# Which idle memory an attention kernel lends to its Exp results, and when it takes it back

## The chip, the cores and the metric

The kernel runs on one core of one Trainium2 chip. The metric is the device time of one execution in microseconds (us). The engines are named as in the profile: PE is TensorE, ACT is ScalarE, DVE is VectorE, POOL is GpSimd, SP is SyncE, whose queue issues most DMAs.

## The reference

Two layers, each an attention block and a feed-forward block with residuals, on x of 2048 tokens by 512, bfloat16. Attention has 32 heads of 16 columns; the feed-forward width is 1792. Both layers use the same weights.

```
def _A_ref(x, wqkv, wo):                     # H = 32, Dh = 16
    q, k, v = split(x @ wqkv)
    scores = einsum("bhqd,bhkd->bhqk", q, k) * Dh ** -0.5
    return reshape(einsum("bhqk,bhkd->bhqd", softmax(scores), v)) @ wo

def _B_ref(x, w1, w2):
    return silu(x @ w1) @ w2

x = x + _A_ref(_layernorm(x), A_wqkv, A_wo)
x = x + _B_ref(_layernorm(x), B_w1, B_w2)
x = x + _A_ref(_layernorm(x), A_wqkv, A_wo)
x = x + _B_ref(_layernorm(x), B_w1, B_w2)
```

## The kernel before

**Tiling.** Queries are cut into four chunks c of 512 tokens, heads into eight blocks hb of four heads. A *segment* is one (layer L, chunk, head block): its scores for 16 blocks of 128 keys. A *tile* is one key block of a segment for two of its four heads, a 128 x 1024 piece of scores in one of three PSUM slots. There are 2 x 4 x 8 x 16 x 2 = 2048 tiles, numbered in order; the planner starts a new "rule" letter every 16 tiles (`STRETCH`).

**One tile.** PE computes its scores (L1306, in the profile `slot<-QT,KT`; 32-row layout), two tiles or one in an issue group. Then there are two ways. (1) ACT takes the Exp from the slot into an Exp buffer (L1530, 128 x 1024 bfloat16), and PE multiplies it with V (L1383, `q_ps<-p,v`, column layout). (2) DVE makes a first power-of-two approximation from the slot (L1564), and three more terms are made from it by adding constants to the bits, on POOL (L1625) or DVE (L1598, called shifts below); the sum of the four terms stands for the Exp. Such a tile needs four buffers and four value matmuls per head instead of one. So a tile can be moved from ACT to DVE, POOL and PE.

**Segments and layers.** The 74 segments are: 32 of the first layer; ten "old" ones of the second layer, which use only the keys of the first three chunks (12 key blocks), because the fourth chunk's feed-forward is not done yet; then the "new" ones that add the missing 4 key blocks, between whole segments of chunk 1; then the rest of chunks 1, 2 and 3. When an old segment closes, DVE copies its unfinished sum out of PSUM (L1199) into `o_old`, rows of 1024 columns in `v_flat`, which held V of the first layer; the new segment of the same head block later rescales it (L499) and adds it (L1203).

**V and its memory.** V of the first layer lies in `v_flat`, V of the second in `x_flat` (8704 columns each, 2176 for a chunk). A V piece (`v_piece`) is 16 matmuls (four per 128 columns of the contraction, in four column groups), an eviction on DVE (L379) and a memset of ones on POOL. `next_pieces` queues the four V pieces of a chunk behind its layer norm once the first layer's feed-forward of this chunk is done.

**The order of the work.** `Flow` is a planner in the kernel's Python. It keeps a clock for each engine, with fixed costs for each kind of instruction, and writes all engines' instructions in the order of its clocks. Background work (keys, queries, V, projections, feed-forward) is cut into `Piece`s of steps with a tile number at which they are due, in four queues; a piece starts only when all pieces in its `after` list are done, and a piece that can't start holds the ones behind it in its queue. PE's turn (`pe_turn`) chooses between scores, values and a background step; when none is possible it may issue a filler matmul (L1423).

**Buffers.** The planner starts with 14 Exp buffers (`NB`). The list `lent` adds others: (first segment, last segment, memory). When segment i begins, `lend` adds the buffers of entries that start at i, and removes those that end at i from the free list; one that is still in use is not given back. ACT's and DVE's turns take the buffer that comes free first. Whether a tile goes to DVE is decided in `want_dve`: among others, when at least `spare` buffers would be free.

```
if sum(b[0] <= at + 600 for b in self.bufs) - self.owed() < self.spare:
    return False
```

**Rule letters.** `RULES` is a string of 128 letters, one for each 16 tiles. Each stands in `KINDS` for seven settings: `spare`, how many value groups may wait (`many`), at how few free buffers values go first (`few`), how many shifts may be queued (`behind`), a factor on the rate of background work (`hurry`), and when DVE helps POOL with shifts (`help`, `wait`). The letter r, with `spare` 99, sends no tile to DVE and speeds background work by 1.5.

Of the kernel before, what the change touches and what calls it, by code (L numbers as in the profile page):

```python
# [20 lines left out]
def kernel(  # L21
# [17 lines left out]
    H = 32  # L39
# [4 lines left out]
    NQC = S // 512  # L44
    FT = F // P
    HB = H // 4
# [3 lines left out]
    VW = DH + 1  # L50
# [77 lines left out]
    v_flat, x_flat = (xpool.tile([P, TT * H * VW], BF16, name=f"v{i}") for i in range(2))  # L128
# [57 lines left out]
    def o_kept(seg):  # L186
        return o_old[seg.hb] if seg.c != 1 else o_more[MORE.index(seg.hb)]
# [46 lines left out]
    def turn(out, in_):  # L234
        turns.append((T_ISSUE, T_LAND))
        nc.sync.dma_start_transpose(out=out, in_=in_)
# [52 lines left out]
    def ln_pieces(c, cell, after):  # L289

        def rs():
            cell["mvb"], cell["rstd"] = ln_scalars(cell["st"])

        def apply(i):
            xn = cell["hT"][:, i, :]
            ln_apply(cell["mvb"], cell["rstd"], i, 4 * c + i, xn)
            turn(xnTs[c][:, :, i * P : (i + 1) * P], xn)

        first = Piece([("sp", 0, rs, "")], after, T_POOL)
        free = [first] + [freed] * (c == 0 and cell.get("L") == 1)  # L300
        return [first, Piece([dve(460, lambda i=i: apply(i), "l") for i in range(4)], free)]
# [27 lines left out]
    def k_piece(L, c, hb):  # L329
        cell = {}  # L330

        def out():
            st = cell["st"] = stpool.tile([P, 512], BF16, name="kq", tag="kq")
            nc.vector.tensor_copy(out=st[:], in_=cell["ps"][:, :])  # L334
            move(kept_q[L, hb, c, :, :], st[:])

        p = Piece(four(
            lambda cts: k_mm(c, hb, cell["ps"][:, :], cts),
            lambda: bank(cell, "k_ps"),
        ) + [dve(700, out, "c"), dve(424, lambda: k_out(c, hb, cell["st"][:]), "l")])  # L340
        p.key = (L, c, hb)
        p.store = Piece([])
        return p
# [31 lines left out]
    def v_piece(tt, L):  # L375
        cell = {}

        def out():
            nc.vector.tensor_copy(  # L379
                out=vs[L][:, tt, :, 0:DH], in_=cell["ps"][:, :].rearrange("p (h d) -> p h d", d=DH)  # L380
            )
            if L:
                ones_v(L, tt, tt + 1)
            v_made.add((L, tt))

        p = Piece(four(
            lambda cts: v_mm(tt, cell["ps"][:, :], cts),
            lambda: bank(cell, "v_ps"),
        ) + [dve(700, out, "c")])
        p.value = (L, tt)  # L390
        return p
# [138 lines left out]
    def heads_piece(oT, seg, attn):  # L530
        alone = seg.c < 2 and (seg.L == 1 or seg.hb < 2)
        alone = alone or (seg.L, seg.c, seg.hb) == (1, NQC - 1, HB - 2)
        k = 0 if alone else seg.hb % 2
        if k == 0:
            at_cell["at"] = opool.tile([P, 4, 2, P], BF16, name="at", tag="at")
        at = at_cell["at"]
        turn(at[:, :, k, :], oT[:])
        if not alone and k == 0:
            return None
        n = 4 * (k + 1)  # L540
        heads = at[:].rearrange("p t s (j w) -> p t (s j) w", j=4)[:, :, 0:n, :]
        cell = {}

        def first():
            cell["rec"] = heads_rec(heads)

        def second():
            heads_mul(heads, cell["rec"], seg.hb - k, attn)

        return Piece([dve(252 if k == 0 else 354, first), dve(536 if k == 0 else 757, second, "l")])  # L550
# [64 lines left out]
    def ffn_pieces(c, emit_out, ln, after):  # L615
# [33 lines left out]
            ))  # L649
        return pieces  # L650

    normed = {}

    def next_pieces(c, L, ln, after):
        ln = ln_pieces(c, ln, after)
        v = [v_piece(4 * c + tq, L) for tq in range(4)]
        normed[c] = ln[-1]
        v[0].after = [ln[-1]]
        return ln + v

    def tail_mm(slots, tq, k):
# [155 lines left out]
    n_old = NQC * HB + HB + len(MORE) - 1  # L817
# [5 lines left out]
    def due(pieces, n):  # L823
        for p in pieces:
            p.due = n
        return pieces
# [88 lines left out]
    def spare(at):  # L915
        made = {}

        def views():
            if not made:
                made["v"] = at()  # L920
            return made["v"]

        return views

    def rows(t, lo, hi):
        return lambda: [
            t[:, 1024 * k : 1024 * k + 1024].rearrange("p (a b) -> p a b", a=2)
            for k in range(lo, hi)
        ]
# [9 lines left out]
    def key_rows():  # L939
        assert with_q[1, NQC - 1, HB - 1].done  # L940
        return [wkq[:, ct, 0 : 2 * D].rearrange("p (a b) -> p a b", a=2) for ct in range(CT)]

    done = n_old + 2 + 2 * HB
    keyed = max(s.i for s in segs if s.kind == "new" and s.c == 0) + 1
    lent = [
        (0, HB, spare(rows(x_flat, 0, 3))),
        (0, 2 * HB, spare(rows(x_flat, 3, 5))),
        (0, 3 * HB, spare(rows(x_flat, 5, 7))),
        (0, 4 * HB, spare(rows(x_flat, 7, 8))),
        (n_old + 3, n_old + HB, spare(idle_hidden)),  # L950
        (n_old + 4, 99, spare(wv_rows)),
        (keyed, 99, spare(key_rows)),
        (done, 99, spare(rows(v_flat, 0, 8))),
    ]

    class Flow:
# [234 lines left out]
        def close(self):  # L1191

            seg = segs[self.open]
            if self.heads is not None:
                self.force(self.heads)
            at = max(self.dve, self.close_at)
            oT = None
            if seg.kind == "old":
                nc.vector.tensor_copy(out=o_kept(seg), in_=self.o_ps[:])  # L1199
            else:  # L1200
                oT = opool.tile([P, 512], BF16, name="oT", tag="oT")
                if seg.kind == "new":
                    nc.vector.tensor_tensor(  # L1203
                        out=oT[:], in0=o_kept(seg), in1=self.o_ps[:], op=ALU.add
                    )
                else:
                    nc.vector.tensor_copy(out=oT[:], in_=self.o_ps[:])
            self.dve = at + 604
            self.o_free = at + 799
            self.close_at = None  # L1210
            self.open += 1
            if self.open == len(segs):
                return oT
            if oT is not None:
                at_ = (seg.L, seg.c)
                if seg.hb == 0:
                    for piece in ends.get((seg.L, seg.c - 2), []):
                        self.force(piece)
                    attns[at_] = apool.tile([P, 4, D], BF16, name="attn", tag="attn")
                piece = self.heads = heads_piece(oT, seg, attns[at_])  # L1220
                land = self.landed(at + 700)
                if piece is not None:
                    piece.ready = land
                    self.bg.append(piece)
                if at_ == (1, NQC - 1) and seg.hb == HB - 3:

                    def early(attn=attns[at_]):
                        for tq in range(4):
                            turn(
                                xnTs[1][:, 0 : CT - 1, tq * P : (tq + 1) * P],  # L1230
                                attn[:, tq, 0 : (CT - 1) * P],
                            )

                    self.turned = Piece([("sp", 0, early, "")], piece)
                    self.qs[2].append(self.turned)
                if seg is more_last:
                    freed.done = True
                if seg.hb == HB - 1:
                    ln = {"L": seg.L}
                    new = epilogue_pieces(seg.c, attns[at_], ln)  # L1240
                    new[0].after = [p for p in (piece, self.fed) if p is not None]
                    ends[at_] = new[-1:]
                    new += ffn_pieces(seg.c, seg.L == 1, ln, new[-1])
                    self.fed = new[-1]
                    if seg.L == 0:
                        new += next_pieces(seg.c, 1, ln, new[-1])
                        if seg.c == NQC - 1:
                            new.append(k_piece(1, seg.c, 0))
                            v_end.append(new[-1])
                    end = {(0, 2): 30, (0, 3): n_old + 1, (1, 0): 66, (1, 1): 69}.get(  # L1250
                        at_, min(seg.i + 1 + HB, len(segs) - 1)
                    )
                    self.qs[1] += self.known(due(new, first[end] - 8))
            return oT
# [413 lines left out]
    }  # L1668
    RULES = (
        "mmmmddddddddddddlllllllldddddddduuuuuuuujjjjuuuullllllllllllllll"  # L1670
        "jjjjjjjjeeeeeeeewwwwwwwwooooooooAAAAAAAAyyyyyyyysssslllloooooooo"
    )
    TAU, NEAR, URGENT, HARD = 700, 300, 4000, 6000
    FROM, TO, EARLY = 0, 99, 300
# [155 lines left out]
```

## Time and profile before

| | us |
|---|---|
| three runs, median | 1598.44 |
| lowest and highest of them | 1597.79, 1599.42 |
| the profiled execution, its own time | 1597.37 |
| its span, first to last instruction | 1595.6 |

The profile has a page of totals, a table of groups of equal instructions (line, engine, operation, tiles, shapes, count | busy us, mean ns of one | idle us before them, and what ended that idle time), lists of waits (who waited for whom: us in total, times, longest us), busy times by stretches of the span, and a timeline of each engine. On ACT, DVE and PE the recorded durations of consecutive instructions overlap, so the step from one start to the next is shorter than a duration. DMA is no matter here:

```profile
HBM read 17.20 MB, written 11.27 MB: 18 GB/s over the span
```

The prediction divides the tiles into eight stages of 256. In the profile of before the first Exp starts at 31.6 us and the last ends at 1551.5; the stages begin at 31.6, 217.8, 404.4, 592.4, 787.7, 989.8, 1181.9 and 1367.7 us.

### The profile page before, as it was taken

What the parts mean: (1) busy time and instruction counts of PE and PEld (TensorE: products, weight loads), DVE (VectorE), ACT (ScalarE), POOL (GpSimd) and SP (SyncE); (2) the same over time, 40 slices, a digit from 0 to 9 for tenths busy, and PEclk for the clock granted to TensorE, in tenths of its full rate; (3) what the DMA queues carried; (4) which work ended last, traced back from release to release, by engine and by line L of the source; (5) the groups of instructions that cost most, each with busy time, mean ns of one, the idle gap of its engine ahead of it and who ended that gap; (6) DMA issues with size and microseconds to landing.
All of it is one profiled execution on the core that took longest, in us unless ns stands there. A gap on an engine that the chain in (4) does not pass through costs nothing.

```text
span 1595.6 us, 41986 instructions
## 1 busy us (share of the span) xinstructions
PE 1523.0 (95%) x17024; PEld 482.7 (30%) x17030; DVE 1253.2 (79%) x1588; ACT 1549.9 (97%) x1761; POOL 1283.5 (80%) x1335
## 2 busy tenths in 40 slices
PE   8999999999999999999999999999999999999998
PEld 3222222223322332233233332232222323323333
DVE  7888888887887777667997458888887698787864
ACT  6999999999999999999999999999999999999993
POOL 3889899997888887767787556897999899888980
PEclk9999999999999999999999999999999999999999
DMA  5011101100110011001111011112100110020010
GB/s 198 21 40 37 30 24 30 24 8 21 30 24 11 11 25 43 11 11 34 57 53 34 14 27 40 27 42 49 27 14 16 33 27 14 16 42 12 17 25 14
DMA packets 105747, 49.28 MB, mean 31 GB/s; under 512 B 79024, under 2 KB 105040, under 8 KB 105552
## 3 DMA queue, kind: packets, MB, share of 16 engines
q1 hardware_dynamic: 103536, 45.51, 11.1%
q8 instruction: 133, 2.18, 0.6%
q10 hardware_dynamic: 2016, 1.08, 0.2%
q14 instruction: 62, 0.51, 0.1%
HBM read 17.20 MB, written 11.27 MB: 18 GB/s over the span
## 4 chain that ended last, share of the span: by engine, by line
PE 51%; ACT 25%; DVE 13%; issue 6%; POOL 3%; DMA 1%; ACTq 0%; DVEq 0%; POOLq 0%
PE slot L1306 18%; ACT p L1530 17%; PE q_ps L1383 14%; PE y_ps L312 7%; PE h_ps L312 4%; ACT v L1530 3%; DVE p L1564 3%; PE k_ps L312 3%; ACT t_sb L595 2%; POOL p L1625 2%; DVE hT L599 1%; PE v_ps L312 1%; ACT wkq L1530 1%; DVE v L1564 1%; DVE p L1598 1%
## 5 line engine op out<-in xcount | busy, mean ns | idle before, releaser
L1530 ACT ACTIVATE p<-slot 128x1024 bf16<-128x1024 f32 x1164 | 1163.5, 1204 | 5.4 <-PE slot L1306 4.6
L1625 POOL TENSOR_TENSOR p<-p,steps 128x512 int32<-128x512 int32 x648 | 684.5, 1078 | 170.5 <-DVE p L1564 151.1
L1306 PE MATMUL slot<-QT,KT 32*128 32x512 bf16 x4096 | 589.5, 381 | 37.8 <-ACT p L1530 24.0
L1383 PE MATMUL q_ps<-p,v 128*17 128x512 bf16 x5002 | 564.3, 381 | 5.5 <-POOL p L1625 1.8
L1564 DVE TENSOR_SCALAR p<-slot 128x1024 uint16<-128x1024 f32 x329 | 401.1, 1219 | 109.0 <-PE slot L1306 93.9
L1306 PEld LDWEIGHTS <-KT 32*128 32x128 bf16 x4096 | 197.7, 91 | 591.2 <-issue 585.1
L1530 ACT ACTIVATE v<-slot 128x1024 bf16<-128x1024 f32 x280 | 316.9, 1203 | 0.3 <-PE slot L1306 0.2
L1383 PEld LDWEIGHTS <-v 128*17 128x17 bf16 x6844 | 161.4, 88 | 283.5 <-issue 230.8
L1383 PE MATMUL q_ps<-v,v 128*17 128x512 bf16 x1214 | 193.1, 381 | 1.0 <-DVE v L1598 0.6
L1625 POOL TENSOR_TENSOR v<-p,steps 128x512 int32<-128x512 int32 x143 | 152.8, 1075 | 25.2 <-DVE p L1564 22.7
L1625 POOL TENSOR_TENSOR p<-v,steps 128x512 int32<-128x512 int32 x145 | 154.4, 1083 | 12.3 <-DVE v L1564 11.0
L312 PE MATMUL h_ps<-xnT,w_sb 128*32 128x512 bf16 x1568 | 132.5, 384 | 7.5 <-DVE hT L599 5.8
L1564 DVE TENSOR_SCALAR v<-slot 128x1024 uint16<-128x1024 f32 x82 | 100.0, 1219 | 25.7 <-PE slot L1306 24.4
L312 PE MATMUL y_ps<-w_sb,hT 128*32 128x512 bf16 x1568 | 116.9, 382 | 0.3
L599 DVE SCALAR_TENSOR_TENSOR hT<-t_sb,h_ps 128x512 bf16<-128x512 f32 x98 | 66.8, 682 | 43.3 <-ACT t_sb L595 43.0
L1530 ACT ACTIVATE wkq<-slot 128x1024 bf16<-128x1024 f32 x80 | 93.5, 1212 | 0.2 <-PE slot L1306 0.2
L312 PE MATMUL k_ps<-xnT,wkq 128*32 128x512 bf16 x960 | 78.6, 384 | 0.7 <-DVE kq L334 0.4
L595 ACT ACTIVATE t_sb<-h_ps 128x512 f32<-128x512 f32 x98 | 75.9, 774 | 0.0
L1598 DVE TENSOR_SCALAR p<-p 128x1024 int16<-128x1024 int16 x98 | 69.6, 713 | 1.0
L1625 POOL TENSOR_TENSOR v<-v,steps 128x512 int32<-128x512 int32 x52 | 56.0, 1081 | 8.8 <-DVE v L1564 8.8
L423 DVE SCALAR_TENSOR_TENSOR QT<-qc,cols,q_ps 128x512 bf16<-128x512 bf16 x74 | 54.7, 739 | 9.6 <-PE q_ps L312 9.0
L1383 PE MATMUL q_ps<-wkq,v 128*17 128x512 bf16 x336 | 60.7, 382 | 0.1
(163 smaller groups left out, 1446.1 us busy)
## 6 DMA issues: line engine op xcount, KB each, us to landing
qc<-kept_q SPq DMA_DIRECT2D x70, 112.0 KB, 2.0
kept_q<-kq SPq DMA_DIRECT2D x60, 128.0 KB, 1.7
w_sb<-in_B_w_dram SPq DMA_DIRECT2D x2, 1792.0 KB, 13.3
out_dram<-x_sb SPq DMA_DIRECT2D x15, 128.0 KB, 1.7
x_sb<-in_A_x_dram SPq DMA_DIRECT2D x3, 512.0 KB, 6.5
old_q<-QT SPq DMA_DIRECT2D x10, 128.0 KB, 1.7
q_was<-old_q SPq DMA_DIRECT2D x10, 128.0 KB, 2.1
at<-oT SPq DMA_TRANSPOSE x63, 2.3
```

The costliest lines, as they stand in the source:

```text
L312: nc.tensor.matmul(ps[g, :], lhsT=lhsT[:, g], rhs=rhs, start=start, stop=stop, skip_group_check=True)
L423: nc.vector.scalar_tensor_tensor(out=dst, in0=qc[:], scalar=own, in1=ps, op0=ALU.mult, op1=ALU.add)
L595: nc.scalar.activation(t_sb, ps, ACT.Tanh, scale=0.5)
L599: nc.vector.scalar_tensor_tensor(out=hT[:, ft, :], in0=t_sb, scalar=1.0, in1=ps, op0=ALU.add, op1=ALU.mult)
L1306: nc.tensor.matmul(self.slots[k][:, jj, :], lhsT=KT[32 * j : 32 * j + KR, t.seg.hb, t.kt * P : (t.kt + 1) * P], rhs=t.seg.QT[32 * j : 32 * ...
L1383: nc.tensor.matmul(self.o_ps[32 * j : 32 * j + VW, :], lhsT=vs[seg.L][:, t.kt, 4 * seg.hb + j, :], rhs=buf[:, jj, :], start=not seg.opened ...
L1530: nc.scalar.activation(buf[:].rearrange("p a b -> p (a b)"), self.slots[x.slot][:].rearrange("p a b -> p (a b)"), ACT.Exp, scale=float(SCALE),
L1564: nc.vector.tensor_scalar(out=whole.bitcast(U16), in0=self.slots[x.slot][:].rearrange("p a b -> p (a b)"), scalar1=float(UNIT), scalar2=fl ...
L1598: nc.vector.tensor_scalar(out=x.bufs[k][1][:].rearrange("p a b -> p (a b)").bitcast(I16), in0=whole.bitcast(I16), scalar1=SHIFTS[k], scala ...
L1625: nc.gpsimd.tensor_tensor(out=b1.bitcast(I32), in0=b0.bitcast(I32), in1=steps32[:, k : k + 1].to_broadcast([P, 512]), op=ALU.add,)
```

## The change

It has four parts.

1. *Lending in the first layer.* Before, eight rows of 1024 columns of `x_flat` were lent from the start and taken back three, two, two and one at the segments 8, 16, 24 and 32. Now each chunk's part of `x_flat` gives two rows, taken back at the segments 12, 20, 28 and 38 (`wanted`). A gate, a `Piece` without steps, stands in the `after` list of each chunk's first V piece, and is set done when the segment `wanted[c]` becomes the open one, that is when all values of the segments before it are issued.
2. *Old results' rows.* When the last segment of the first layer closes, the rows 1 to 7 of `v_flat` are lent; row hb is taken back at the start of segment 32 + hb, whose old result goes there. When a new segment of chunk 0 closes, its row is lent again. Before, all eight rows were lent at segment 59.
3. *The idle hidden tile.* The seven buffers in `hT`'s memory, lent at segment 44, are taken back at segment 52 in place of 49.
4. *Rule letters.* 64 of the 128 letters are set anew, in pairs, 36 of them for tiles up to 1024.

The number of buffers in hand is then 22 to tile 384, 20 to 640, 18 to 896, 16 to 1024 and 23 just after it (then one less with each segment to 38, where three more go), where it was 22 to tile 256, 19 to 512, 17 to 768, 15 to 1024 and 14 after it.

```diff
+    wanted = [HB * (c + 1) + HB // 2 for c in range(NQC - 1)] + [NQC * HB + HB - 2]
+    gates = [Piece([]) for c in range(NQC)]
...
-        v[0].after = [ln[-1]]
+        v[0].after = [ln[-1], gates[c]]
...
-    done = n_old + 2 + 2 * HB
     keyed = max(s.i for s in segs if s.kind == "new" and s.c == 0) + 1
+    def new_v_rows(c):
+        return rows(x_flat[:, 4 * H * VW * c : 4 * H * VW * (c + 1)], 0, 2)
+
+    old_o = [spare(rows(v_flat, hb, hb + 1)) for hb in range(HB)]
     lent = [
-        (0, HB, spare(rows(x_flat, 0, 3))),
-        (0, 2 * HB, spare(rows(x_flat, 3, 5))),
-        (0, 3 * HB, spare(rows(x_flat, 5, 7))),
-        (0, 4 * HB, spare(rows(x_flat, 7, 8))),
-        (n_old + 3, n_old + HB, spare(idle_hidden)),
+        *((0, wanted[c], spare(new_v_rows(c))) for c in range(NQC)),
+        *((99, NQC * HB + hb, old_o[hb]) for hb in range(1, HB)),
+        (n_old + 3, keyed - 1, spare(idle_hidden)),
         (n_old + 4, 99, spare(wv_rows)),
         (keyed, 99, spare(key_rows)),
-        (done, 99, spare(rows(v_flat, 0, 8))),
     ]
...
+            if self.open in wanted:
+                gate = gates[wanted.index(self.open)]
+                gate.done, gate.ready = True, self.pe
+            if seg.i == NQC * HB - 1:
+                self.bufs += [(self.pe, b) for hb in range(1, HB) for b in old_o[hb]()]
+            if seg.kind == "new" and seg.c == 0:
+                self.bufs += [(self.dve, b) for b in rows(v_flat, seg.hb, seg.hb + 1)()]
...
-        "mmmmddddddddddddlllllllldddddddduuuuuuuujjjjuuuullllllllllllllll"
-        "jjjjjjjjeeeeeeeewwwwwwwwooooooooAAAAAAAAyyyyyyyysssslllloooooooo"
+        "mmmmddssvvooddllppeeddnnllpphhqqeeuuuunnppjjuullxxkkllllllllllll"
+        "jjrrlleeeeeexxbbwwwwwwwwoobbnnkkllAAAAzzssvvyyyyqqsslllllloooooo"
```

## The prediction

> **What bounds the kernel now.** I read the busy times first, then the same by stages, then the instructions of ACT (ScalarE) in order of time, then who waits for whom.
>
> The page, busy time by engine:
>
> ```profile
> PE 1523.0 (95%) x17024; PEld 482.7 (30%) x17030; DVE 1253.2 (79%) x1588; ACT 1549.9 (97%) x1761; POOL 1283.5 (80%) x1335
> ```
>
> Two engines are almost full. The stages tell them apart (columns: stretch, length, then busy us and count of PE, PEld, DVE, ACT, POOL, granted clock, DMA share, GB/s). Here are the stretch before the first Exp, two of the eight stages, and what follows the last Exp:
>
> ```profile
> 0.00:31.60 31.60, 25.26 (x145) 11.64 (x148) 25.50 (x66) 18.82 (x31) 11.80 (x42) 1.00 0.72 250
> 989.80:1181.90 192.10, 181.71 (x1933) 56.49 (x1927) 160.70 (x210) 189.68 (x215) 168.35 (x165) 1.00 0.15 34
> 1367.70:1551.50 183.80, 180.37 (x2134) 55.71 (x2131) 144.25 (x164) 183.42 (x207) 168.96 (x168) 1.00 0.10 23
> 1551.50:1595.60 44.10, 36.53 (x193) 15.22 (x190) 18.80 (x39) 17.35 (x33) 0.86 (x1) 1.00 0.05 16
> ```
>
> From 31.6 to 1551.5 us ACT is busy to a few tenths of a us per stage, at the full clock. PE still has 3.4 us free in the fullest stage here and 10.4 us in the other, and its records overlap. So the bound is the number of ACT instructions times their step, plus what ACT loses. The timeline of ACT gives the step (columns: start, us, engine, line; a merged row holds several):
>
> ```profile
> 504.23 2.19 ACT L1530 ACTIVATE p<-slot 128x1024 bf16<-128x1024 f32 x2
> 506.04 1.29 ACT L1530 ACTIVATE v<-slot 128x1024 bf16<-128x1024 f32 x1
> 506.96 3.12 ACT L1530 ACTIVATE p<-slot 128x1024 bf16<-128x1024 f32 x3
> 510.48 1.02 ACT L1530 ACTIVATE p<-slot 128x1024 bf16<-128x1024 f32 x1 [0.40 <-PE slot L1306]
> 511.40 0.59 ACT L595 ACTIVATE t_sb<-h_ps 128x512 f32<-128x512 f32 x1
> 511.88 3.85 ACT L1530 ACTIVATE p<-slot 128x1024 bf16<-128x1024 f32 x4
> ```
>
> A row's own 1.02 to 1.29 us is not the step, since instructions overlap. From 504.23 to 506.04 two Exps take 1.81 us: **0.905 us each**; from 511.40 to 511.88 a Tanh takes 0.48 us. The program has 1590 Exps and 108 short ones (98 Tanh and 10 factors f_sb) in this stretch: 1590 x 0.905 + 108 x 0.48 = 1490.8 of 1519.9 us. The other 29 us are what ACT loses. Which waits make them? The groups of ACT name the idle part:
>
> ```profile
> L1530 ACT ACTIVATE p<-slot 128x1024 bf16<-128x1024 f32 x1164 | 1163.5, 1204 | 5.4 <-PE slot L1306 4.6 <-PE q_ps L1383 0.2
> L1530 ACT ACTIVATE v<-slot 128x1024 bf16<-128x1024 f32 x280 | 316.9, 1203 | 0.3 <-PE slot L1306 0.2
> L1530 ACT ACTIVATE wv_sb<-slot 128x1024 bf16<-128x1024 f32 x46 | 55.1, 1213 | 1.1 <-PE slot L1306 1.1
> ```
>
> With the groups of wkq and idle (0.2 and 0.3 us), 7.3 us are idle, nearly all until scores came from PE; 2.1 of them are the first two gaps of the run. Only 0.2 us is a wait for readers of a buffer (q_ps L1383). The other 22 us are starts late by less than the overlap hides. **So no wait for a buffer is there to be removed.** More buffers can help only through the planner, which gives a tile to DVE (VectorE) only when enough are free (`want_dve`), and may order PE better.
>
> **The change part by part**, from the two programs' orders of instructions.
>
> 1. *Exps.* 1590 become 1586; DVE takes 462 tiles where it took 458. By stages of 256 tiles the Exps change by 0, +1, 0, -2, 0, 0, -1, -2; the short instructions stay 108. Price of one: 0.905 us in a packed run, or 0.926 by the first eighth of the tiles (31.6 to 217.8 us: 186.2 us for 201 Exps and nothing else, stalls included). 4 x 0.905 to 0.926 = 3.6 to 3.7 us; I take **-3.6 us**, since the lost time has a term of its own. This is a small sum for so many buffers: writes into V's rows rise from 280 to 405 Exps and fall elsewhere. The loan is used, but most of it only replaces other buffers.
>
> 2. *What DVE and POOL take over.* DVE: 4 first passes x 1.22 us (L1564) and 18 more shifts (185 to 203) x 0.71 us (L1598) = 17.7 us; it is idle 342 us. POOL (GpSimd): 6 fewer shifts (1189 to 1183) x 1.08 us (L1625) = -6.5 us. Cost on the path: nothing, while both have room in each stage; POOL is tightest at the end, 14.8 us free of 183.8. If that cover went, see the third rival.
>
> 3. *PE.* 24 more value matmuls (4 tiles x 3 more terms x 2). In issue groups: 16 more score groups, 11 fewer value groups, 40 more changes between the row and the column layout (2701 to 2741). Neighbouring groups of one kind start 0.22 us apart and those across a change 0.32, so 5 x 0.22 + 40 x 0.10 = +5.1 us. It lies on PE's free 72.6 us: most falls in the first eighth (+2.4) and the sixth (+2.6, against 10 us free). In the last quarter, where PE is fullest, it is +0.7. Bounds: 0 to +5.1; I take 0, because PE is where ACT is the one waited for, as PE's waits show (us in total, times, longest):
>
> ```profile
> PE slot L1306 <- ACT p L1530: 24.0, 91, 1.0
> ```
>
> 4. *The gates on V's pieces.* A gate opens when its chunk's lent rows are no longer read, at tiles 390, 643, 902 and 1171. The pieces' evictions (L379) stand at tiles 508 to 523, 755 to 772, 959 to 972 and 1230 to 1245 before, and at 502 to 522, 750 to 765, 965 to 972 and 1228 to 1246 after. Every gate opens at least 50 tiles early, some 37 us at 0.74 us a tile (1519.9 / 2048), so no instruction stands behind one on any engine, and SP's queue is as long as before (316). Cost: **0**. Without that cover, four pieces of 16 matmuls and 0.69 us eviction each would be late, 4 x (4 x 0.22 + 0.69) = 6.3 us.
>
> 5. *The old results' rows.* They are lent after the last value matmul of the first layer and taken back before their own segment starts; the copy into them (L1199, 0.69 us, 8 times) comes a segment (18 us) later. The rows of hT (idle) go back at segment 52 in place of 49, before the next hT is made. No row of the profile has a wait there; each between 0 and 10 x 0.69 = 6.9 us, and I take 0.
>
> 6. *Stalls of ACT.* The order decides them. The largest after the start, 1.06 us idle at 1061.21, is a late query: the scores of tile 1376 start at 1060.68, behind their segment's query, which DVE (L423, from 1059.89) could only write after a multiply of 1.52 us (L499). One issue group of PE stands between the query and its scores there; in the new order 20 do, so this stall goes. The next one of the kind, 0.59 us idle at 1110.62 (tile 1440, one group between), stays as it is. Against this, the new order has two runs of 2.4 us of PE work between score groups (11 groups at tiles 256 and 1504); the seven of 2.2 us in the old order cost ACT 0 to 0.15 us each, so such a run costs 0 to 0.6, say 0.3: -1.06 + 2 x 0.3 = **-0.5 us**. For the rest I take no change; bounds -5 us (all idle time but the first two gaps goes) to +5 us (as much is added).
>
> 7. *The ending.* One unit of the last projection that ran between the last tiles now runs behind them: one matmul of 0.38 us at most, half hidden: **+0.2 us**.
>
> **Sum**: -3.6 - 0.5 + 0.2 = -3.9 us. The profiled execution took 1597.37 us (span 1595.6 and 1.8 around it), 1.07 below the median of the three runs, 1598.44. The same difference gives 1593.5 beside the profiled execution and **1594.5** as the median to expect, 0.24% faster. Below 0.2% (3.2 us) a measurement of this kernel can't tell a change from none.
>
> **The rivals.**
>
> *Fewer stalls as well* (0.22). With 13 to 20 free buffers at an Exp's turn where there were 7 to 12 (by the planner's lists, tiles 1024 to 1150 and 1344 to 1470) the order waits less, and ACT's idle 5 us go too: -3.6 - 5 = -8.6, some **1590**. For it: the old order loses most in tiles 1344 to 1470. Against: none of those waits names a buffer, and this stage runs no fewer Exps.
>
> *Nothing to measure: POOL held up* (0.22). The shift on DVE takes 0.36 to 1.32 us by its own rows, in one shape, so something holds it. Nine of the 18 added shifts lie in tiles 1664 to 2047, where POOL is fullest: 9 x 0.71 = 6.4 us of POOL's free time. If POOL waits for all of it, its shifts come late, their values too, and segments close late: -3.6 + 6.4 = +2.8, **1601.2**; half of that is 1598. Against: POOL has 14.8 us free there, and PE waited only 1.8 us for POOL in the whole run. The Trainium skill (SBUF — State Buffer, Who interferes with whom) says that VectorE in a two-port mode and GpSimd take one shared port pair by an exclusive lock, and the loser blocks for the whole instruction. The trace agrees as far as DVE's spread shows it; by that rule alone the time would be this rival's.
>
> *Slower: PE becomes the bound* (0.13). Its place is each stretch where PE has no free time before the score groups: tiles 1600 to 2047, and the first eighth, where nine more groups stand. If PE's +5.1 us is exposed whole and the Exps' gain is lost behind it: **1603.5**. It decides once the added 0.10 us per layout change comes straight before scores that ACT waits for. For it: ACT's idle time ends on PE's scores. Against: PE itself waits 24 us for ACT at just those score groups, and the fullest quarter gets only 0.7 us.
>
> **Chances and range.** The forecast (1592.5 to 1596.5) has 0.43, of which 0.28 lies below 1595.2. Faster by over 0.2%: 0.28 + 0.22 = 0.50. Within 0.2%: 0.15 of the forecast and 0.22 of POOL's rival, 0.37. Slower: 0.13. The range leaves out a tenth at each side: 1589.5, just under the fewer-stalls case, to 1601.5, just over POOL's bound.
>
> **What would show it.** Right: ACT has 1586 Exps, the stretch from first to last Exp is near 1516 us, idle before L1530 near 7 us, no wait of DVE v L379 for PE q_ps. The stalls' rival: that idle falls toward 3 us. POOL's: POOL's rows lengthen beyond 1.08 us and PE q_ps waits for POOL well over 1.8 us. PE's: ACT's waits for PE slot grow and PE's for ACT shrink. The forecast fails if ACT's lost 29 us move by more than 4 either way.

## The result, and the profile after

The changed kernel takes 1603.04 us (median of 11 runs, 1600.57 to 1606.55) beside 1597.99 (11 runs, 1596.86 to 1600.49): ratio **1.0031**, 95% interval 1.0021 to 1.0041. It is slower by 5 us, where 3.9 us less was forecast; the measured time lies above the range.

The busy times of the profiled execution (its own time 1601.63 us, span 1599.8):

```profile
PE 1523.7 (95%) x17051; PEld 480.6 (30%) x17051; DVE 1279.9 (80%) x1610; ACT 1549.0 (97%) x1757; POOL 1280.7 (80%) x1329
```

ACT's busy time fell by 0.9 us, POOL's by 2.8; DVE's rose by **26.7 us**. The stages, with the same columns as before the change: the first, two that grew most, and what follows the last Exp. The first two rows are the first and the seventh stage of the kernel before.

```profile
31.60:217.80 186.20, 179.16 (x1996) 52.63 (x1996) 159.56 (x198) 184.90 (x201) 160.28 (x156) 1.00 0.10 31
1181.90:1367.70 185.80, 181.36 (x2110) 55.95 (x2108) 148.90 (x177) 185.80 (x213) 168.14 (x166) 1.00 0.09 21
```

```profile
31.80:220.10 188.30, 181.18 (x2004) 53.64 (x1999) 163.06 (x197) 185.63 (x202) 160.55 (x156) 1.00 0.11 30
991.70:1185.90 194.20, 180.76 (x1912) 54.72 (x1910) 172.24 (x220) 191.05 (x216) 163.78 (x160) 1.00 0.14 34
1185.90:1374.00 188.10, 183.25 (x2142) 55.53 (x2138) 153.11 (x182) 185.50 (x213) 168.02 (x165) 0.99 0.08 21
1556.20:1599.80 43.60, 36.44 (x190) 15.12 (x182) 18.19 (x38) 17.34 (x33) 0.00 (x0) 1.00 0.04 13
```

From the first Exp to the last it takes 1524.4 us instead of 1519.9, with four Exps fewer; the ending is 0.5 us shorter. By the usual steps in the two traces, 0.904 us an Exp and 0.478 a short instruction, **ACT lost 30.9 us before and 39.0 after**. The excess sits in three stages: the first (186.2 to 188.3 us, as many Exps), the sixth (192.1 to 194.2, as many) and the seventh (185.8 to 188.1, one Exp fewer). The other five changed by 0.4 us or less beside their Exps.

The groups of ACT: idle before them is 12.6 us in all, 7.3 before the change, and PE's scores end it.

```profile
L1539 ACT ACTIVATE p<-slot 128x1024 bf16<-128x1024 f32 x1042 | 1054.7, 1188 | 9.8 <-PE slot L1315 7.9 <-PE k_ps L312 0.4 <-ACT idle L1539 0.2
L1539 ACT ACTIVATE v<-slot 128x1024 bf16<-128x1024 f32 x405 | 451.6, 1184 | 2.0 <-PE slot L1315 1.7
```

What held PE? For each Exp that began over 0.25 us late (the first two aside) I looked for idle stretches of PE from 1.5 us before the Exp was due, and for what ended the longest. Before the change 28 such Exps are 13.0 us late together, and 17 of them (8.2 us) follow a wait of PE for DVE; after it 39 are 20.2 us late, and **29 (14.3 us) follow a wait for DVE**. Two more (2.2 us) follow a DMA. With stretches over 0.15 us alone it is 17 before and 26 (13.1 us) after. From the first Exp to the last, PE's own waits of over 0.15 us for DVE grow from 19.3 to 23.7 us, and those for DMAs from nothing to 2.4.

The costliest place shows how DVE comes to be late. It is the timeline of the changed kernel from 1275 us; L227 applies the layer norm to four blocks, L236 transposes them by DMA, and PE's hidden matmuls need them:

```profile
1275.20 1.03 POOL L1634 TENSOR_TENSOR p<-p,steps 128x512 int32<-128x512 int32 x1
1275.26 4.26 DVE L227 TENSOR_SCALAR hT<-x_sb,sc 128x512 bf16<-128x512 bf16 x4 [0.60 <-POOL sc L223]
...
1276.19 1.09 POOL L1634 TENSOR_TENSOR v<-v,steps 128x512 int32<-128x512 int32 x1
1276.41 5.45 SPq L236 DMA_TRANSPOSE xnT<-hT  x4
1277.24 1.08 POOL L1634 TENSOR_TENSOR p<-v,steps 128x512 int32<-128x512 int32 x1
...
1278.29 1.09 POOL L1634 TENSOR_TENSOR wkq<-v,steps 128x512 int32<-128x512 int32 x1
...
1283.26 0.61 PE L312 MATMUL h_ps<-xnT,w_sb 128*32 128x512 bf16 x8 [1.50 <-DMA xnT<-hT]
1283.78 1.03 POOL L1634 TENSOR_TENSOR p<-p,steps 128x512 int32<-128x512 int32 x1
1283.80 0.60 PE L1315 MATMUL slot<-QT,KT 32*128 32x512 bf16 x2
...
1284.44 1.02 ACT L1539 ACTIVATE p<-slot 128x1024 bf16<-128x1024 f32 x1 [1.26 <-PE slot L1315]
```

Four POOL shifts and four DVE operations go in step: each of the four takes a whole shift, 1.07 us, where it takes 0.41 alone (below). So the last transpose lands late, PE stands 1.5 us before the hidden matmuls, the scores queued behind them come late, and ACT stands 1.26 us. Just behind this pause the granted clock falls to 0.5 for 3.41 us (from 1283.8 us), and the scores take 0.60 instead of 0.39 us.

Of the 472 DVE operations of this kind (one SBUF input: L321, L227, L406, L414, L1607) 356 began while a POOL shift ran. All of them ended behind it, 334 by less than 0.35 us: 0.085 to 0.285 us in the median, by line. The 472 are 18 more than before, and took 347.8 us in place of 330.0.

### The profile page after: what moved, and what is told of

Read it like the earlier page. It is cut to its first block, busy times and chain, and to the rows that moved or that the text cites. A ratio compares the mean times of both kernels' runs of the same rounds, so it can differ in the third digit from the quotient of the medians.

```text
span 1599.8 us, 41978 instructions
## 1 busy us (share of the span) xinstructions
PE 1523.7 (95%) x17051; PEld 480.6 (30%) x17051; DVE 1279.9 (80%) x1610; ACT 1549.0 (97%) x1757; POOL 1280.7 (80%) x1329
## 3 DMA queue, kind: packets, MB, share of 16 engines
q10 hardware_dynamic: 2016, 1.08, 0.2%
## 4 chain that ended last, share of the span: by engine, by line
PE 55%; ACT 21%; DVE 14%; issue 6%; POOL 3%; DMA 2%; ACTq 0%; DVEq 0%; POOLq 0%
PE slot L1315 19%; PE q_ps L1392 16%; ACT p L1539 13%; PE y_ps L312 7%; ACT v L1539 4%; PE h_ps L312 4%; DVE p L1573 3%; PE k_ps L312 2%; ACT t_sb L595 2%; DVE v L1573 1%; DMA at<-oT 1%; POOL p L1634 1%; PE v_ps L312 1%; DVE hT L599 1%; PE q_ps L312 1%
## 5 line engine op out<-in xcount | busy, mean ns | idle before, releaser
L1539 ACT ACTIVATE p<-slot 128x1024 bf16<-128x1024 f32 x1042 | 1054.7, 1188 | 9.8 <-PE slot L1315 7.9
L1634 POOL TENSOR_TENSOR p<-p,steps 128x512 int32<-128x512 int32 x509 | 537.5, 1075 | 125.3 <-DVE p L1573 111.5
L1315 PE MATMUL slot<-QT,KT 32*128 32x512 bf16 x4096 | 593.9, 382 | 37.5 <-ACT p L1539 19.4
L1392 PE MATMUL q_ps<-p,v 128*17 128x512 bf16 x4454 | 533.6, 382 | 4.3 <-DVE p L1573 1.4
L1539 ACT ACTIVATE v<-slot 128x1024 bf16<-128x1024 f32 x405 | 451.6, 1184 | 2.0 <-PE slot L1315 1.7
L1573 DVE TENSOR_SCALAR p<-slot 128x1024 uint16<-128x1024 f32 x303 | 369.1, 1218 | 79.9 <-PE slot L1315 75.3
L1392 PE MATMUL q_ps<-v,v 128*17 128x512 bf16 x1752 | 276.8, 381 | 1.1 <-ACT v L1539 0.4
L1634 POOL TENSOR_TENSOR v<-p,steps 128x512 int32<-128x512 int32 x220 | 235.8, 1081 | 42.2 <-DVE p L1573 23.4
L1634 POOL TENSOR_TENSOR p<-v,steps 128x512 int32<-128x512 int32 x188 | 201.1, 1088 | 24.1 <-DVE v L1573 22.5
L1573 DVE TENSOR_SCALAR v<-slot 128x1024 uint16<-128x1024 f32 x114 | 138.9, 1219 | 28.9 <-PE slot L1315 27.3
L423 DVE SCALAR_TENSOR_TENSOR QT<-qc,cols,q_ps 128x512 bf16<-128x512 bf16 x74 | 54.7, 739 | 14.3 <-PE q_ps L312 13.3
L1607 DVE TENSOR_SCALAR p<-p 128x1024 int16<-128x1024 int16 x81 | 59.7, 740 | 0.9
L312 PEld LDWEIGHTS <-hT 128*32 128x32 bf16 x2016 | 40.8, 95 | 57.9 <-issue 42.0
```

The lines of the kernel that those rows point to most:

```text
L312: nc.tensor.matmul(ps[g, :], lhsT=lhsT[:, g], rhs=rhs, start=start, stop=stop, skip_group_check=True)
L423: nc.vector.scalar_tensor_tensor(out=dst, in0=qc[:], scalar=own, in1=ps, op0=ALU.mult, op1=ALU.add)
L1315: nc.tensor.matmul(self.slots[k][:, jj, :], lhsT=KT[32 * j : 32 * j + KR, t.seg.hb, t.kt * P : (t.kt + 1) * P], rhs=t.seg.QT[32 * j : 32 * ...
L1392: nc.tensor.matmul(self.o_ps[32 * j : 32 * j + VW, :], lhsT=vs[seg.L][:, t.kt, 4 * seg.hb + j, :], rhs=buf[:, jj, :], start=not seg.opened ...
L1539: nc.scalar.activation(buf[:].rearrange("p a b -> p (a b)"), self.slots[x.slot][:].rearrange("p a b -> p (a b)"), ACT.Exp, scale=float(SCALE),
L1573: nc.vector.tensor_scalar(out=whole.bitcast(U16), in0=self.slots[x.slot][:].rearrange("p a b -> p (a b)"), scalar1=float(UNIT), scalar2=fl ...
```

## The experiments

Theory S: DVE's operations on SBUF wait for POOL's shifts, so the order, planned with fixed costs, comes late on the chip, and the new letters suffer more from it. Rivals: the lent memory itself (M), the clock (C), PE or DMAs (O), the letters alone (L), DVE's own work (V).

### One part alone

The changed kernel's buffers with the letters of before; then the buffers of before with the new letters.

```diff
# e1_lend_only: the change without its RULES
-        "mmmmddssvvooddllppeeddnnllpphhqqeeuuuunnppjjuullxxkkllllllllllll"
...
+        "mmmmddddddddddddlllllllldddddddduuuuuuuujjjjuuuullllllllllllllll"
...
# e2_letters_only: of the change its RULES alone
```

> The changed kernel's buffers, gate and returns, with the rule letters of before. Theory P (the time is lost where the fixed order holds PE behind something that comes later than the planner's costs say; letters are fitted to one set of buffers): much slower, about 1620 to 1630 us, with ACT standing still for several us at a few segment starts whose query is late. Rival L (the loan is good in itself and the new letters harm): at or below 1598 us. Rival M (the lent memory itself costs waits): slower by some us, spread over all Exps.

> The buffers of before with the new rule letters. Theory P: much slower again, about 1620 to 1635 us, at segment starts, since these letters were fitted to other buffers. Rival L (letters harm, buffers help): slower than the changed kernel by about what the loan gives, 2 to 5 us, about 1605 to 1608 us. Rival M (the lent memory costs waits): faster than the changed kernel, near 1598 us.

Measured: 1632.28 us (ratio 1.0217, 1.0204 to 1.0230) and 1636.48 us (1.0233, 1.0219 to 1.0248). Both are some 2 us above the ranges of theory P (an early form of S), and far from those of L and M. A letter set is fitted to one set of buffers, and each half alone leaves queries late. Most of this loss is not P's, though: the planner's own clock ends some 28 and 31 us later for these two than for the kernel before, so that only 7 and 8 us of the measured 34.8 and 39.0 come from a chip that is later than the plan. The timeline of ACT in the first of them shows one such start:

```profile
986.30 1.33 ACT L1539 ACTIVATE p<-slot 128x1024 bf16<-128x1024 f32 x1
998.33 1.02 ACT L1539 ACTIVATE p<-slot 128x1024 bf16<-128x1024 f32 x1 [10.69 <-PE slot L1315]
```

These two do not tell what each part is worth, since a half without the other costs more than the whole change moves.

### PE filled where it waits

```diff
# e3
 def a(ft=ft, hc=hc):
     bank(hc, "h_ps")
+    for _ in range(6 if ft == 0 else 0):
+        for j in range(4):
+            nc.tensor.matmul(hc["ps"][32 * j : 32 * j + DH, :], lhsT=wkq[:, 0, 2 * D : 2 * D + DH],
+                rhs=wo_sb[:, 0, :], start=True, stop=True, skip_group_check=True)
```

> The changed kernel in the same order, with 24 filler matmuls (16 columns, no DMA behind them) into the bank of a chunk's first hidden block ahead of the matmuls that wait for the transposes of the normed rows (7 chunks). Theory C (PE idles there, its clock is halved for a window of 3.4 us, and that is most of the loss): granted clock 1.000 and 1599 to 1600.5 us. Theory P alone (the halved clock only follows): 1601 to 1604 us as before, or up to 3 us more where the fillers come in the way.

> The changed kernel once more, for a second profile and more times. Theory C: runs with a granted clock of 1.000 take about 1600.5 us, and each window at half clock adds 1.3 to 2 us, so that the times follow the clock; the windows lie where PE waits in order behind a DMA or DVE. Theory P alone: times without relation to the clock.

Measured: the fill takes 1608.74 us (1.0071, 1.0059 to 1.0083); the repeat 1602.85 us (1.0037, 1.0023 to 1.0050). The fill kept the clock up in the stage around 1283 us, yet two windows at half clock came elsewhere (1114.9 and 1176.4 us), and ACT lost 46.2 us: fillers in seven chunks cost more than they keep, and the time is above both ranges. The repeat lost 38.4 us, in the same stages as the first profile to 0.3 us each, but for two (the sixth and the last, 0.3 and 0.5 less), with its window at 1284.5: the loss belongs to the order, not to chance.

Theory C has a share. Over the 17 runs of the changed kernel in these two jobs the time follows the mean granted clock: 1600.6 and 1601.0 us at 1.000, a median of 1601.6 at 0.999 (7 runs) and 1606.1 at 0.996 (4). The kernel before has 35 of its 75 runs at 1.000, median 1597.4, and 1599.3 at 0.998 (24). So at the full clock the change costs some 3.4 us (two runs of the changed kernel show it), and the rest goes with windows at half clock.

### POOL unloaded

```diff
# e5 (on before.py), e6 (on after.py); "seen" holds the buffers written whole so far
+            w = 64 if id(x.bufs[k][1]) in self.seen else 512
...
             nc.gpsimd.tensor_tensor(
-                out=b1.bitcast(I32), in0=b0.bitcast(I32),
-                in1=steps32[:, k : k + 1].to_broadcast([P, 512]), op=ALU.add,
+                out=b1.bitcast(I32)[:, 0:w], in0=b0.bitcast(I32)[:, 0:w],
+                in1=steps32[:, k : k + 1].to_broadcast([P, w]), op=ALU.add,
```

> The kernel before, same order, but POOL's shift (1.08 us) works on 64 of 512 columns once a buffer has been written whole, so that most added terms are stale in seven eighths of their columns: POOL is nearly unloaded and DVE's SBUF operations no longer wait for it. Theory S (DVE's and POOL's SBUF operations hold each other up, and that makes the order late): DVE's shift falls from 0.74 to about 0.42 us mean, ACT's loss from 31 to some 22 us, time about 1588 to 1592 us. Rival O (the loss is in PE's order and DMAs): 1596 to 1598 us.

> The changed kernel with the same cut of POOL's shift. Theory S: the changed order loses no more than the old one when POOL is unloaded, so this is 2 to 5 us below the same cut of the kernel before (four Exps fewer, 3.6 us). Rival O: it stays 2 to 5 us above it.

Measured: **1592.38 us** for the old order (ratio to the kernel before 0.9963, 0.9949 to 0.9977) and **1589.39 us** for the new one (0.9944, 0.9931 to 0.9957); the five runs of each don't overlap (1591.7 to 1594.3, 1588.5 to 1591.1). The first is 0.4 us above S's range. With POOL unloaded the changed order is 3.0 us faster, near the 3.6 us of the forecast's four Exps. ACT loses 25.6 and 25.9 us, and of the Exps that are late behind DVE 2 and 3 are left (0.8 and 1.8 us). PE's waits for DVE fall to 13.1 and 10.5 us. PE's waits for POOL itself, the other thing that a shorter shift could remove, were only 1.8 and 0.5 us in the uncut kernels. Three groups of DVE, first in the kernel before (behind the count: busy us, mean ns of one):

```profile
L321 DVE TENSOR_SCALAR KT<-kq,cols 128x512 bf16<-128x512 bf16 x60 | 46.0, 767 | 2.2
L227 DVE TENSOR_SCALAR hT<-x_sb,sc 128x512 bf16<-128x512 bf16 x44 | 37.5, 878 | 3.5 <-POOL sc L223 3.5
L521 DVE TENSOR_TENSOR attn<-at,rec 128x256 bf16<-128x256 bf16 (+1 forms) x42 | 37.2, 885 | 1.0
```

In the changed kernel as it is:

```profile
L321 DVE TENSOR_SCALAR KT<-kq,cols 128x512 bf16<-128x512 bf16 x60 | 48.4, 806 | 2.1
L227 DVE TENSOR_SCALAR hT<-x_sb,sc 128x512 bf16<-128x512 bf16 x44 | 38.8, 910 | 5.0 <-POOL sc L223 5.0
L521 DVE TENSOR_TENSOR attn<-at,rec 128x256 bf16<-128x256 bf16 (+1 forms) x42 | 42.7, 1016 | 1.1
```

And in e6, the same kernel with POOL's shifts cut to 64 of 512 columns:

```profile
L321 DVE TENSOR_SCALAR KT<-kq,cols 128x512 bf16<-128x512 bf16 x60 | 25.0, 417 | 2.1
L227 DVE TENSOR_SCALAR hT<-x_sb,sc 128x512 bf16<-128x512 bf16 x44 | 16.6, 408 | 4.5 <-POOL sc L223 4.4
L521 DVE TENSOR_TENSOR attn<-at,rec 128x256 bf16<-128x256 bf16 (+1 forms) x42 | 24.6, 586 | 1.1
```

The same operations take about half as long; all of DVE falls from 1279.9 to 1104.2 us. S's first half holds (DVE's waits for POOL make the order late), and O falls: PE's order and DMAs are the same in both.

### Other letters

The next eight kernels set letters anew, searched for a short end of the planner's own clock. Six keep the rest of the code; e9 and e10 also change how the planner prices a DVE operation and a POOL shift that meet (the port, in the expectations).

```diff
# e7 and e11, e12: before.py; e8, e13, e14: after.py; RULES (both lines joined)
e7  wwnniijjvvddjjuulllllllljjddddddoooogghhggjjuuuugguuAAggjjllllllhhhhCChheeeeeeaannttyyyyCCCCkkAAssbbvvllxxmmCCjjllccccuuwwwwBBnn
e8  wwoohhttddllggggppeeddwwllpphhqqeeuummnnuuccccppxxkkllllpphhppssjjrrggggtteexxbbnnnnnnnnAAeeAAllllBBeezzsseeyyAAoooohhoowwwwCCCC
e11 mmwwgghhcccccccclllllllliiiiccppooooCCooddCCuuuuppppppppqqllaaaaaanniiiikkeewweeCCddyywwggwwqqooxxAAAAAACCxxwwyysssshhhheellzzoo
e12 zzeejjbbeeeejjjjllllllllddddddddCCooCCoouujjuuuuiiiisshhkklljjmmiillwwppeeuueeiiCCBBBBoollkkmmppxxooAAxxAAnnzzyyjjddllllyyzzoooo
e13 mmeecciissvvaaeegguuiizzAAppAAqqCCCCCCCCppkkuullxxkkllaahhhhaauunnrrAAvvkkeexxbbyyyyyyyyoobbyykkllAAAAzzssvvwwyyqqsslllllloooobb
e14 zzeehhssvvhhAAyyuueehhAAwwpphhqqeeuuwwmmpphhAAvvxxkkjjAAttqqBBccxxrruupptteexxbbnnnnyyyyBBddllllllAAAAzzssvvxxyyqqssqqllllnnookk
# e9 (on before.py), e10 (on after.py), with letters of their own: a DVE step on SBUF
-                    at = max(at, self.lock)
-                    self.held_port = at + ns - PIPE + 20
-                end = at + ns
+                end = at + ns
+                if at < self.lock:
+                    end = max(end, self.lock + 40 + 150)
+                    self.held_port = self.lock + 40 + 85
...
```

> The buffers of before, no gate, with other rule letters, searched for a short plan by the planner's own clock, unchanged; 1585 Exps instead of 1590, so 4.5 us of ACT less, as the changed kernel has 3.6 us less. Theory S (letters chosen by a planner that prices DVE's SBUF operations wrongly don't hold on the chip, whatever the buffers): no faster than before, 1598 to 1605 us, ACT loses 36 us or more. Rival M (it is the lent memory that costs): 1592 to 1595 us.

> The changed kernel's buffers with letters searched on by the same unchanged planner's clock; 1583 Exps, 6.3 us of ACT less than before. Theory S: again 1598 to 1606 us. Rival W (the changed kernel just had unlucky letters): 1590 to 1595 us.

> The buffers of before; the planner's price of a DVE operation on SBUF that meets a POOL shift is set to what the traces show (it ends 0.15 us after the shift, 0.285 for a shift on DVE, and POOL's next shift starts 0.085 us later, where the planner let DVE start after the shift and held POOL until DVE was done), and the letters are searched for that clock; 1567 Exps, 20.8 us of ACT less. Theory S: 1575 to 1590 us. Rival O: at or above 1598 us, since PE takes over.

> The same with the changed kernel's buffers and gate; 1560 Exps, 27 us of ACT less than before. Theory S: 1568 to 1585 us and below the same with the buffers of before, so that the loan is worth something once the planner prices the port. Rival M: not below it.

Measured: e7 1598.21 us (1.0001, 0.9991 to 1.0011), e8 1606.69 (1.0055, 1.0038 to 1.0072), e9 1609.36 (1.0065, 1.0050 to 1.0080), e10 1616.39 (1.0113, 1.0097 to 1.0129). e8 is 0.7 us above S's range and far from W's. Two errors of mine are in these kernels. The search ended with the last tile, so it pushed 28 to 56 matmul steps of background work behind it: after the last Exp they take 50.3, 53.4, 50.6 and 57.7 us, the kernel before 44.1. Without the longer ending, 6.2 us, e7 would lie at 1592.0, in M's range, and its ACT lost 32.2 us where S gave 36 or more; so e7 does not speak for S, though its time lies in S's range. And the new price of the port missed its aim by 20 us and more: the planner then gave DVE and POOL more tiles (1567 and 1560 Exps), DVE was busy 1298.0 and 1315.3 us, and ACT lost 54.9 and 60.9 us. The numbers given for O (e9) and M (e10) hold, those of S do not. The price itself was off: it holds POOL 0.085 us, where the traces show nothing to 0.18 us, by line (last section). S's other half, that the plan fails because it prices these meetings wrongly, is therefore not shown; the old planner does charge DVE for them, as it starts a DVE operation only behind the shift. Where plan and chip part stays open.

Four more sets, with all work counted to the end:

> The buffers of before, planner unchanged, letters searched for the planner's clock at the end of all work, what is left after the last tile included: 4.0 us less than the kernel before by that clock, 1589 Exps. Theory M (the lent memory, or the plans that more buffers allow, bring the loss): the clock's gain shows, 1592 to 1597 us. Theory S (any letters set anew by this planner lose several us to DVE's late operations): 1599 to 1604 us.

> Another such search with the buffers of before: 6.0 us less by the planner's clock, 1587 Exps. Theory M: 1590 to 1595 us. Theory S: 1597 to 1603 us.

> The changed kernel's buffers and gate, letters searched in the same way: 6.5 us less than the kernel before by the planner's clock, 1586 Exps. Theory M: 7 to 9 us above the clock's gain, as the changed kernel is, 1599 to 1602 us, and above both searches with the buffers of before. Theory S: 1597 to 1603 us, among them.

> Another search with the changed kernel's buffers: 8.6 us less by the planner's clock, 1583 Exps. Theory M: 1597 to 1600 us, above both searches with the buffers of before. Theory S: 1595 to 1602 us, among them.

Measured: e11 1596.45 us (0.9991, 0.9982 to 0.9999), e12 1600.18 (1.0014, 1.0005 to 1.0023), e13 1598.01 (0.9999, 0.9990 to 1.0008), e14 1602.72 (1.0029, 1.0019 to 1.0040). Neither theory has all four: e11 lies where M puts it, e12 where S does, e13 in S's range and below M's, e14 above both. Measured less planned is +9.0 us for the changed kernel, and +7.0, +6.8, +13.6 for the other sets on its buffers (e8, e13, e14), but -1.0, +2.7 and +8.5 on the buffers of before (e7, e11, e12); of the two halves above, e1 has the changed buffers (+7) and e2 those of before (+8). The planner's gain is mostly lost on both lists; that more buffers add to the loss is likely but not shown, as the groups overlap and their sets were searched to different depth. e11 is the best of them, by less than the 0.2% that a measurement can tell.

### DVE's own work, and another order

In e15 the cut of the POOL experiment is made in DVE's shifts, 128 of 1024 columns; in e16 POOL's shifts are cut in e14's order.

```diff
# e15; "seen" holds the buffers written whole so far
+                w = 128 if id(x.bufs[k][1]) in self.seen else 1024
...
                 nc.vector.tensor_scalar(
-                    out=x.bufs[k][1][:].rearrange("p a b -> p (a b)").bitcast(I16),
-                    in0=whole.bitcast(I16), scalar1=SHIFTS[k], scalar2=None, op0=ALU.add,
+                    out=x.bufs[k][1][:].rearrange("p a b -> p (a b)").bitcast(I16)[:, 0:w],
+                    in0=whole.bitcast(I16)[:, 0:w], scalar1=SHIFTS[k], scalar2=None, op0=ALU.add,
```

> The changed kernel, same order, POOL's shifts whole, but DVE's shifts (203) work on 128 of 1024 columns once a buffer has been written whole, so their other columns are stale. Theory S (what makes DVE late is waiting for the POOL shift that is under way, whatever its own work): a DVE shift that meets a POOL shift still ends 0.2 to 0.3 us behind it, the mean falls from 0.73 to only 0.5 or so, and the time stays at 1599 to 1603 us. Rival V (DVE just has more work of its own): 0.3 us saved on each of 203 shifts counts, 1592 to 1597 us.

> The second searched letter set with the changed kernel's buffers, which took 1602.7 us, same order, with POOL's shifts cut to 64 of 512 columns as in the two cut kernels before. Theory S: with POOL unloaded the planner's gain shows, 1592.4 us of the cut kernel before less 8.6 us, 1582 to 1586 us. Rival O (this order loses elsewhere): 1590 to 1597 us.

Measured: e15 1598.37 us (1.0001, 0.9992 to 1.0011), e16 **1585.97 us** (0.9924, 0.9907 to 0.9940). The second is S's number. The first lies between: the shifts keep 0.46 to 0.49 us in their largest groups, with an eighth of the columns, because they wait for POOL, as S says (the shortest of them takes 0.18 us); but DVE's busy time falls by 51 us to 1228.6, POOL's by 33, and some 4.6 us of the loss go, which V says. So both count, DVE's own operations and their waits for POOL.

The orders side by side (one profile each; the fill and the repeat of the changed order left out):

| kernel | Exps | DVE busy us | ACT lost us | median us |
|---|---|---|---|---|
| e16, e14's order, POOL cut | 1583 | 1108.0 | 24.2 | 1585.97 |
| e5, before, POOL cut | 1590 | 1089.7 | 25.6 | 1592.38 |
| e6, changed, POOL cut | 1586 | 1104.2 | 25.9 | 1589.39 |
| before | 1590 | 1253.2 | 30.9 | 1597.99 |
| e11 | 1589 | 1259.5 | 31.5 | 1596.45 |
| e7 | 1585 | 1265.0 | 32.2 | 1598.21 |
| e15, changed, DVE's shifts cut | 1586 | 1228.6 | 35.0 | 1598.37 |
| e8 | 1583 | 1280.0 | 35.9 | 1606.69 |
| e13 | 1586 | 1268.2 | 36.4 | 1598.01 |
| e12 | 1587 | 1264.4 | 37.1 | 1600.18 |
| changed | 1586 | 1279.9 | 39.0 | 1603.04 |
| e14 | 1583 | 1271.7 | 40.7 | 1602.72 |
| e9 | 1567 | 1298.0 | 54.9 | 1609.36 |
| e10 | 1560 | 1315.3 | 60.9 | 1616.39 |
| e1, the buffers alone | 1583 | 1272.2 | 71.5 | 1632.28 |
| e2, the letters alone | 1595 | 1249.7 | 72.0 | 1636.48 |

The last two lose most at stalls that were in the plan, whatever DVE does. In the other orders more busy time of DVE goes with more loss of ACT: below 1110 us the loss is 24 to 26 us, from 1228 to 1280 it is 31 to 41, above 1298 it is 55 and more. Within the middle group the order is not kept, and DVE's busy time holds its waits for POOL, so the table alone shows no cause.

## Why the prediction was wrong, by its steps

- *What bounds the kernel, the step of an Exp* (part 1): right, though ACT was not busy to a few tenths of a us in each stage: in the sixth it was idle for 2.4 us. Four Exps fewer are worth 3 us once nothing else interferes (e5, e6).
- *What DVE and POOL take over* (part 2): **the step that failed.** "Cost on the path: nothing, while both have room in each stage." DVE had 342 us of idle time, but its first pass is what frees a PSUM slot, and its evictions and queries stand before PE's next group in a fixed order; an average share says nothing of when they come. The 17.7 us that I counted became 26.7 us of busy time, as operations that did not change grew longer (L521 from 885 to 1016 ns, the largest share, L321 from 767 to 806, L227 from 878 to 910), and ACT lost 8.1 us more than before where nothing was counted. POOL's load was needed for it: with POOL's shifts cut in both orders, the changed one loses only 0.3 us more.
- *PE* (part 3): the +5.1 us stayed covered; PE's idle time even rose, from 72.6 to 76.1 us.
- *The gates, the old results' rows, the ending* (parts 4, 5, 7): right. DVE's wait before L379 is 15.4 us where it was 15.3, no row waits for the lent rows, and the ending is 0.5 us shorter where 0.2 more was written.
- *Stalls* (part 6): the named ones came about as said: the stall at tile 1376 is gone, and of the two long PE runs one made ACT 0.44 us late, the other less than 0.25. "For the rest I take no change; bounds -5 to +5" was the wrong part: the rest rose by some 9 us, outside its bounds.
- *The rivals.* POOL's rival saw the right place and the wrong loser. I had read DVE's spread of 0.36 to 1.32 us as a threat to POOL; POOL's shift stayed at 1.08 us, PE's waits for POOL fell from 1.8 to 0.5 us, and DVE waits. The Trainium skill (SBUF — State Buffer, Who interferes with whom) says that who takes the shared pair first keeps it for its whole instruction. The trace agrees, with DVE ending behind the shift in 356 of 472 cases; but an L321 that takes 0.41 us alone ends 0.15 us behind, so that part of it falls inside the shift's record. PE's rival had the sign and, by luck, a time near the result, 1603.5; its mechanism fails: unloading POOL, with PE's order unchanged, removes the loss. Its signature (ACT's waits for PE's scores grow, PE's for ACT shrink: 24.0 to 19.4 us) can't tell it from DVE holding PE.

What stays open is how much of the loss the larger set of buffers brings, how much any new letter set would, and why the order of before suffers less from the same waits.

## What to carry to other kernels

Where a static order keeps one engine 97% busy, price a change by the lateness it gives to the next engine in the chain, which works in a fixed order, not by the idle time of the helper. An operation with two usual durations (here 0.41 or 1.07 us) belongs in the sum at its longer one, with a loss on the path as its bound. When a planner's own clock promises 0.3%, compare it with the clock's error between orders on the chip, here -1 to +14 us, before believing the sign. A cut that unloads one engine in both orders tells in two runs whether the difference comes from it.

## What the runs showed of the hardware

- A DVE operation with bfloat16 operands in SBUF that begins during a POOL shift ends 0.085 (L414), 0.15 (L321, L227, L406) or 0.285 us (L1607) behind it in the median; 334 of 356 ended within 0.35 us. POOL's next shift then takes 1.03 us behind an L414, 1.09 behind an L321, L227 or L406 and 1.22 behind an L1607, where one that follows no such meeting takes 1.03. Most of the cost falls on DVE: its busy time fell by 175.7 us when POOL's shifts were cut (e6), POOL's by 33 when DVE's were (e15).
- While the kernels run, the granted clock is halved for 3.41 us or a multiple (6.83, 13.65). A pause of PE of 1.5 us and a gap of 0.4 us shortly before it were followed by this at 1283 us; pauses of 1.5 and 1.6 us in other runs were not (e1 at 1141.9, e12 at 1103.9 us). So not every such pause of an order is hit. The times of the changed kernel spread more, 6 us between its runs and 3.6 us before; that this comes from the clock alone is not shown.
